# Corner order in the small products, and three bank sets in place of four in chunk 0, of an attention and SiLU-MLP kernel

## The chip, the cores and the metric

The kernel runs on one core of one Trainium2 chip. The metric is the device time of one execution in microseconds (us), as the median of several runs.

## The reference

Two stages follow each other. The first is linear attention: softmax of q over the features of a head, softmax of k over the sequence, and two products without any further softmax. Its output, with the heads side by side, is the input x of a two-layer network with SiLU between the layers.

```python
batch, n_heads, seq, head_dim = (8, 8, 576, 64)
q_s = softmax(q, axis=-1); k_s = softmax(k, axis=2)
kv  = np.einsum('bhsd,bhse->bhde', k_s, v)        # 64 x 64 per head
att = np.einsum('bhsd,bhde->bhse', q_s, kv)
x   = att.transpose(0, 2, 1, 3).reshape(4608, 512)
h   = x @ w_in                                     # 512 -> 2048
g   = h * (1.0 / (1.0 + np.exp(-h)))
out = g @ w_out                                    # 2048 -> 512
```

## The kernel before

**Tiling.** The 4608 rows of x are worked in chunks t. Chunk 0 is the 576 rows of batch 0; chunk 1 has 448 rows (64 more of its second product are copied from chunk 0); chunks 2 to 8 have 512. A chunk goes through three steps: the attention of its batch (b), the first product with W1 and SiLU into GT, and the second product with W2 into the output tile ow. From chunk 1 on the first product is made with a seven-product (Strassen) scheme, `group(t, g, i)`, and from chunk 1 on so is the second one, `prod(t, i, m)`. Chunk 0 is made plainly: the first product by `wide_mm` and `wide_silu`, one feature block of 128 at a time (fb 0 to 15), the second by `mm2_plain`, four matmuls for each of 16 steps. Eight feature blocks of chunk 1 are made plainly too, by `mm1`.

**Attention.** `exp_q`, `qsum`, `qnorm` make the softmax of q, `exp_k` the exponentials of k, `vcast` puts v into `vaug` with a column of ones beside each head, so that `kv` gives the product and the normalizing sum at once. q is transposed by TensorE (`tr`, `trcopy`) for batches 0 and 1, by a DMA (`q_transpose`) afterwards. The tiles of `kv` and `xt_mm` are 64x64: each matmul uses one of the four corners of the 128x128 array, with r and s choosing the half of the input partitions and the half of the output partitions. `kv` (line 189) makes 72 matmuls of 65 columns for a batch, in 18 rounds of four corners. `kvcopy` scales them into `kvn`; `xt_mm` (line 228) makes x's products, four corners for each piece, and `xt_evac` copies them from PSUM into XT.

**Memory for sums.** PSUM has eight banks, in the tile PS. Chunk 0's first product takes two banks for a feature block, banks 2 * (fb % 4) and the next: four sets. `wide_silu` reads them twice: ScalarE makes a tanh (line 250) into sg, VectorE multiplies (line 251) into GT. `mm2_plain` adds up in banks 2 to 5; `mm2_plain_out(0, m)` copies bank 2 + m out (lines 418 and 420). The groups of chunk 1 use banks 0, 1 and 6, 7, those of later chunks banks 0, 1 and 2, 3. `mm1` has one bank for a feature block.

**Order.** Everything is issued in an order written out by hand (`manual_schedule`). TensorE's work is a list `units`; `plan(u, f)` puts other work in front of unit u, so each engine's queue gets its instructions in the order in which the units are walked. After chunk 0's 16 `wide` units, from b1 on, come the units of `mm2_plain` (b0, "b"), then pairs of these with chunk 1's groups (gs, "g") by the string `four_pairs`, then eight `mm1` units, then chunk 2 (`full(2)`).

```python
    units += [b0.pop(0) for _ in range(10)]
    units += [{"b": b0, "g": gs}[x].pop(0) for x in four_pairs[:-1]]
    units += [lambda i=i: mm1(1, FB[i], (i + 2) % 4) for i in range(HF)]
```

**Loads.** W1, W2 and batch 1 are loaded on POOL's queue, in the order of the program; batch 0 and the batches from 3 on, and the stores, on SP's. A small POOL copy, `gate`, reads the first k load of batch 0 before W1 is loaded, and a second one (line 566) reads W1's second load before batch 1's q is. W1 comes in five loads: two halves (of input rows, c) of feature blocks 0 to 3, then blocks 4 to 7, 8 to 11 and 12 to 15.

Of the kernel before, what the change touches and what calls it, by code (L numbers as in the profile page):

```python
# [17 lines left out]
def kernel(  # L18
# [9 lines left out]
    nc = tc.nc  # L28
    B, H, S, D = q.shape
# [3 lines left out]
    J = S // P  # L33
    NG = H // 2
    NC = DM // 128
    NFB = DFF // 128
    HF = NFB // 2
    TCH = 512
# [66 lines left out]
    def exp_q(b, cc, g0=0, g1=2):  # L105
        if "eq" not in st[b]:
            st[b]["eq"] = ap.tile([128, J, NG * D], BF16, name="eq")
        nc.scalar.activation(  # L108
            out=half(st[b]["eq"], cc)[:, :, g0:g1], in_=jgd(b, "qt", cc)[:, :, g0:g1], func=ACT.Exp
        )  # L110

    def exp_k(b, cc):
        nc.scalar.activation(out=half(ek, cc), in_=jgd(b, "kt", cc), func=ACT.Exp)  # L113
# [30 lines left out]
    def qsum(b, cc, gs=None):  # L144
        new_zq(b)
        z, e = st[b]["zq"][:, cc], half(st[b]["eq"], cc)
        if gs is None:
            nc.vector.reduce_sum(out=z, in_=e, axis=AX.X)  # L148
        else:
            nc.vector.reduce_sum(out=z[:, :, gs], in_=e[:, :, gs, :], axis=AX.X)  # L150
        if gs != 0:
            nc.vector.reciprocal(out=st[b]["rzq"][:, cc], in_=z)  # L152
# [19 lines left out]
    def tr(b, cc, j0, j1, bank):  # L172
        t = PS[:, bank, :].bitcast(BF16)
        for j in range(j0, j1):
            nc.tensor.transpose(
                out=t[:, (j - j0) * 128:(j - j0 + 1) * 128],
                in_=st[b]["eq"][:, j, cc * 128:(cc + 1) * 128],
                identity=ident,
            )

    def trcopy(b, cc, j0, j1, bank, eng=nc.vector):
        t = PS[:, bank, :].bitcast(BF16)[:, 0:(j1 - j0) * 128].rearrange("x (j y) -> x j y", y=128)
        copy(eng, new_qt(b)[:, j0:j1, cc, :], t)

    def kv(b, cc):
        for j in range(J):
            for r in range(2):
                for s in range(2):
                    nc.tensor.matmul(  # L189
                        out=PS[s * 64:(s + 1) * 64, 6 + r, cc * 128:cc * 128 + E1],  # L190
                        lhsT=ek[r * 64:(r + 1) * 64, j, (2 * cc + s) * D:(2 * cc + s + 1) * D],
                        rhs=vaug[r * 64:(r + 1) * 64, j, 2 * cc + s, :],
                        start=(j == 0),
                        stop=(j == J - 1),
                    )
# [13 lines left out]
    def kv_both(b):  # L209
        kv(b, 0)  # L210
        kv(b, 1)
        kvcopy(b)
# [9 lines left out]
        return got  # L222

    def xt_mm(b, cc, col, n, bank, dst):
        for r in range(2):
            for s in range(2):
                h = slice(s * 64, (s + 1) * 64)
                nc.tensor.matmul(  # L228
                    out=PS[r * 64:(r + 1) * 64, bank + s, dst:dst + n],
                    lhsT=kvn[b % 3][h, cc, r, :],  # L230
                    rhs=st[b]["qT"][h, col // P:(col + n) // P, cc, r * 64:(r + 1) * 64],
                )
# [5 lines left out]
    def xt(t, cc, eng=nc.scalar):  # L238
        got = pieces(t)
        for b, col, n, dst in got:  # L240
            xt_mm(b, cc, col, n, 6, dst)
        xt_evac(t, cc, 6, got[0][3], TCH, got[0][3], eng)
# [12 lines left out]
    def wide_mm(fb, cs, ns=range(2)):  # L255
        for c in cs:
            for n in ns:
                nc.tensor.matmul(  # L258
                    out=PS[:, 2 * (fb % 4) + n, 0:S // 2],
                    lhsT=W1[:, c, fb * 128:(fb + 1) * 128],  # L260
                    rhs=XTS[0][:, c, n * (S // 2):(n + 1) * (S // 2)],
                    start=(c == 0),
                    stop=(c == NC - 1),
                )

    def wide_silu(fb):
        bank = 2 * (fb % 4)
        silu(
            0, fb, PS[:, bank:bank + 2, 0:S // 2],
            GTS[0][:, fb, :].rearrange("p (a n) -> p a n", a=2), S,  # L270
        )
# [12 lines left out]
    def mm1(t, fb, bank):  # L284
        o0 = pieces(t)[0][3]
        mm1_mm(t, fb, bank, range(NC))
        nc.scalar.activation(  # L287
            out=GTS[t % 2][:, fb, o0:TCH], in_=PS[:, bank, o0:TCH], func=ACT.Silu, scale=1.0 / XS
        )
# [21 lines left out]
    def ws_op(i, g):  # L311
        w, f0, f1 = WS[g], 4 * g + 8, 4 * g
        in0, in1, op = {
            1: (wa(0, f1), wa(1, f1), ALU.add),
            2: (w[0], wa(0, f0), ALU.subtract),
            3: (wa(0, f0), wa(0, f1), ALU.subtract),
            4: (wa(1, f0), w[1], ALU.subtract),
        }[i]
        nc.vector.tensor_tensor(out=w[i - 1], in0=in0, in1=in1, op=op)

    def xs_op(t, i):
        x = [xs[:, :, 0:width(t)] for xs in XS4]
        in0, in1 = {
            1: (xb(t, 0, 1), xb(t, 0, 0)),
            2: (xb(t, 1, 1), x[0]),
            3: (xb(t, 1, 1), xb(t, 0, 1)),
            4: (xb(t, 1, 0), x[1]),
        }[i]
        nc.vector.tensor_tensor(out=x[i - 1], in0=in0, in1=in1, op=ALU.subtract)
# [114 lines left out]
    def t_op(i, eng, f0=0, f1=HF):  # L444
        o, in0, in1 = {
            1: (T1, B12, B11),
            2: (T2, B22, T1),
            3: (T3, B22, B12),
            4: (T4, B21, T2),
        }[i]  # L450
        f = slice(f0, f1)
        eng.tensor_tensor(out=o[:, f], in0=in0[:, f], in1=in1[:, f], op=ALU.subtract)
# [91 lines left out]
    def load_w1(f0, f1, c0=0, c1=NC):  # L544
        nc.gpsimd.dma_start(
            out=W1[:, c0:c1, f0 * 128:f1 * 128],
            in_=w_in[c0 * 128:c1 * 128, f0 * 128:f1 * 128].rearrange("(c p) f -> p c f", p=128),
        )
# [12 lines left out]
    load_w1(0, 4, 0, 2)  # L561
    load_w1(0, 4, 2, 4)
    load_w1(4, 8)
    load_w1(8, 12)
    load_w1(12, 16)
    nc.gpsimd.tensor_copy(gate, W1[0:1, 2, 0:1])
    load(1, "qt", q, 0, nc.gpsimd)
    load(1, "qt", q, 1, nc.gpsimd)
    load_w2(0, 4)
# [36 lines left out]
    xt_evac(0, 1, 6, 0, 320, 0, nc.scalar)  # L606
    xt_evac(0, 1, 2, 0, 256, 320, nc.vector)
    wide_mm(1, (0, 1))
    wide_mm(2, (0, 1))


    units = []
# [2 lines left out]
    def plan(u, f):  # L615
        at.setdefault(u, []).append(f)

    def wide(fb):
        wide_mm(fb, range(2 if fb < 3 else 0, NC))
        wide_silu(fb)  # L620

    for fb in range(NFB):
# [19 lines left out]

    b0 = [lambda i=i: mm2_plain(0, i) for i in range(NFB)]
    gs = [lambda i=i: group(1, 1, i, None, True) for i in ORDER]
    units += [b0.pop(0) for _ in range(10)]
    units += [{"b": b0, "g": gs}[x].pop(0) for x in four_pairs[:-1]]
    units += [lambda i=i: mm1(1, FB[i], (i + 2) % 4) for i in range(HF)]
    assert not (b0 or gs)

    def full(t):  # L650
# [117 lines left out]
    plan(13, lambda: (exp_q(1, 1, 1, 2), qsum_pair(1, 1), qnorm(1, 0, nc.gpsimd)))  # L768
    plan(14, lambda: (load(2, "qt", q, 0, nc.gpsimd), load(2, "qt", q, 1, nc.gpsimd)))
    plan(b1 + 2, lambda: (exp_k(1, 0), exp_k(1, 1)))  # L770
    plan(b1 + 4, lambda: (tr(1, 0, 0, 5, 6), tr(1, 0, 5, J, 7)))
    plan(b1 + 4, lambda: (trcopy(1, 0, 0, 5, 6, nc.scalar), trcopy(1, 0, 5, J, 7)))
    plan(b1, lambda: (qsum_end(1, 1), qnorm(1, 1, nc.vector)))
    plan(b1, lambda: load_w2(12, 16))
    plan(b1 + 9, lambda: nc.scalar.copy(out=GTS[1][:, :, 0:64], in_=GTS[0][:, :, TCH:S]))
    plan(b1 + 3, lambda: (load(2, "kt", k, 0, nc.gpsimd), load(2, "kt", k, 1, nc.gpsimd)))
    plan(b1 + 6, lambda: (load(2, "vt", v, 0, nc.gpsimd), load(2, "vt", v, 1, nc.gpsimd)))
    plan(b1 + 4, lambda: vcast(1, 0, nc.scalar))
    plan(b1 + 5, lambda: (tr(1, 1, 0, 5, 0), tr(1, 1, 5, J, 1)))
    plan(b1 + 5, lambda: (vcast(1, 1, nc.scalar, 0, 1), vcast(1, 1, nc.vector, 1, 2)))  # L780
    plan(b1 + 6, lambda: (trcopy(1, 1, 0, 5, 0, nc.scalar), trcopy(1, 1, 5, J, 1)))
    plan(b1 + 8, lambda: kv_both(1))
    plan(b1 + 9, lambda: xt(1, 0))
    plan(b1 + 10, lambda: xt(1, 1))

    plan(b1 + 3, lambda: (ws_op(1, 1), ws_op(2, 1)))
    plan(b1 + 4, lambda: ws_op(3, 1))
    plan(b1 + 6, lambda: ws_op(4, 1))
    plan(b1 + 9, lambda: t_op(1, nc.vector))
    plan(b1 + 11, lambda: (xs_op(1, 1), ws_op(1, 0)))  # L790
    plan(b1 + 11, lambda: (xs_op(1, 2), xs_op(1, 3), xs_op(1, 4)))
    plan(b1 + 11, lambda: exp_q(2, 0))
    plan(b1 + 12, lambda: (qsum(2, 0, 0), qsum(2, 0, 1), qnorm(2, 0, nc.gpsimd)))
    plan(b1 + 14, lambda: exp_q(2, 1))
    plan(b1 + 15, lambda: exp_k(2, 0))
    plan(b1 + 15, lambda: (qsum(2, 1, 0), qsum(2, 1, 1), qnorm(2, 1, nc.gpsimd)))
    plan(b1 + 16, lambda: q_transpose(2))
    plan(b1 + 18, lambda: exp_k(2, 1))
    plan(b1 + 18, lambda: (vcast(2, 0, nc.gpsimd), vcast(2, 1, nc.gpsimd)))
    plan(b1 + 22, lambda: (group_silu(1, 2, 4, 1), group_silu(1, 0, 12, 0)))  # L800
    plan(b1 + 19, lambda: t_op(2, nc.vector))
    plan(b1 + 23, lambda: [load(3, x, y, i, nc.sync) for x, y, i in (
        ("qt", q, 0), ("kt", k, 1), ("kt", k, 0), ("vt", v, 0), ("vt", v, 1), ("qt", q, 1)
    )])
    plan(b1 + 22, lambda: mm2_plain_out(0, 0, nc.vector))
    plan(b1 + 22, lambda: mm2_plain_out(0, 1, nc.vector))
    plan(b1 + 24, lambda: group_silu(1, 1, 12, 1))
    plan(b1 + 14, lambda: ws_op(2, 0))
    plan(b1 + 24, lambda: (t_op(4, nc.vector), ws_op(3, 0)))
    plan(b1 + 25, lambda: kv_both(2))  # L810
    plan(b1 + 26, lambda: ws_op(4, 0))
# [41 lines left out]
```

## Time and profile before

| what | value |
| --- | --- |
| median of 5 runs | 263.81 us (263.69 to 264.52) |
| the profiled execution's own time | 263.75 us |
| its span, first to last instruction | 262.0 us |
| mean granted TensorE clock | 0.999 |
| TensorE matmuls busy | 252.7 us (96%) |
| VectorE, ScalarE, POOL busy | 208.3, 187.1, 67.8 us |
| 576 k-v matmuls (line 189), one of them | 193 ns (median) |
| 128 of x's products (line 228), one of them | 294 ns (median) |

An instruction's row has its own duration; matmuls are pipelined, so many are in flight at once, and what a group of them costs is read from the start of its first one to the start of the next group. PE is TensorE, DVE is VectorE, ACT is ScalarE. "Idle before" an instruction comes with what ended the wait. Line numbers L... are those of the kernel before; in the changed kernel, lines behind `kv` move by one, and behind `xt_mm` by two up to the loads of W1.

### The profile page before, as it was taken

To read this page: it belongs to the slowest core of one execution; us is meant where nothing else is said; L and a number is where in the kernel's file an instruction comes from. 1 tells how busy PE (TensorE), PEld (TensorE's weight loads), DVE (VectorE), ACT (ScalarE), POOL (GpSimd) and SP (SyncE) were. 2 spreads that over 40 slices of the span, in tenths; PEclk is the share of its full clock that TensorE was granted. 3 is DMA by queue.
4 is the path that set the end of the run, shared out by engine and by line. 5 is a ranking of instruction groups with operands and counts; after the bars stand their busy time and mean duration, and the time that the engine had idled before them with its cause. 6 is when DMAs were issued, how large, how long until landed. Compare 5 with 4: busy or idle time off the path is not lost.

```text
span 262.0 us, 6411 instructions
## 1 busy us (share of the span) xinstructions
PE 252.7 (96%) x2732; PEld 203.1 (78%) x2732; DVE 208.3 (80%) x269; ACT 187.1 (71%) x211; POOL 67.8 (26%) x63
## 2 busy tenths in 40 slices
PE   8899999999999999999999999999999999999992
PEld 3467655755888888888888888888888888888881
DVE  2957897897997999799979997999798548855832
ACT  4857976897995799579957995799574748484610
POOL 1664790650560306030603060306000000000003
PEclk9999999999999999999999999999999999999999
DMA  7999999679979486957794869540434003400634
GB/s 249 337 194 297 300 325 336 237 159 334 372 292 217 124 220 237 180 158 191 267 225 116 221 236 181 160 94 3 90 72 91 3 0 67 95 3 1 137 66 120
DMA packets 35964, 45.89 MB, mean 175 GB/s; under 512 B 16208, under 2 KB 21008, under 8 KB 35936
## 3 DMA queue, kind: packets, MB, share of 16 engines
q1 hardware_dynamic: 29568, 33.69, 46.9%
q0 software_dynamic: 6128, 11.60, 17.1%
q8 instruction: 21, 0.34, 0.5%
q10 hardware_dynamic: 240, 0.20, 0.2%
q14 instruction: 7, 0.06, 0.1%
HBM read 36.70 MB, written 9.44 MB: 176 GB/s over the span
## 4 chain that ended last, share of the span: by engine, by line
PE 76%; DMA 8%; DVE 8%; ACT 2%; POOL 2%; issue 2%; SPq 0%; POOLq 0%; DVEq 0%; ACTq 0%
PE PS L468 34%; PE PS L368 32%; PE PS L405 4%; DMA qt<-in_q_dram 4%; DMA kt<-in_k_dram 2%; DMA W<-in_moe_w_in_dram 2%; PE PS L228 2%; PE PS L276 2%; PE PS L189 2%; DVE h L346 1%; DVE S L442 1%; DVE zq L148 1%; DVE GT L442 1%; DVE GT L251 1%; POOL out_dram L732 1%
## 5 line engine op out<-in xcount | busy, mean ns | idle before, releaser
L346 DVE TENSOR_TENSOR h<-PS,h 128x1024 f32<-128x1024 f32 (+1 forms) x45 | 53.9, 1199 | 13.4 <-ACT h L89 7.5
L468 PEld LDWEIGHTS <-GT 128*128 128x128 f16 x512 | 49.6, 98 | 6.9 <-issue 1.2
L368 PEld LDWEIGHTS <-WS 128*128 128x128 f16 x480 | 46.8, 98 | 6.8 <-issue 0.7
L468 PE MATMUL PS<-W,GT 128*128 128x256 f16 x384 | 49.1, 273 | 0.0
L368 PE MATMUL PS<-XS,WS 128*128 128x256 f16 (+1 forms) x360 | 46.3, 272 | 0.1
L352 ACT ACTIVATE GT<-h 128x1024 f16<-128x1024 f32 (+1 forms) x45 | 46.1, 1047 | 0.3 <-DVE h L346 0.3
L89 ACT COPY h<-PS 128x1024 f32<-128x1024 f32 (+1 forms) x35 | 35.1, 1004 | 14.1 <-PE PS L368 13.6
L157 POOL TENSOR_TENSOR eq<-eq,rzq 128x1152 bf16<-128x1152 bf16 x13 | 27.7, 2135 | 55.5 <-DVE rzq L152 55.5
L468 PEld LDWEIGHTS <-S 128*128 128x128 f16 x384 | 37.1, 98 | 5.6 <-issue 1.0
L368 PEld LDWEIGHTS <-W 128*128 128x128 f16 x360 | 34.7, 98 | 5.5 <-issue 1.3
L468 PE MATMUL PS<-T,S 128*128 128x256 f16 x256 | 32.7, 273 | 0.2 <-ACT h L89 0.2
L368 PE MATMUL PS<-XT,W 128*128 128x256 f16 (+1 forms) x240 | 29.6, 272 | 0.5 <-ACT GT L287 0.3
L352 ACT ACTIVATE GT<-PS 128x1024 f16<-128x1024 f32 (+1 forms) x15 | 15.3, 1017 | 18.9 <-PE PS L368 18.9
L91 POOL CAST vaug<-vt 128x1152 bf16<-128x1152 f32 x12 | 16.4, 1370 | 45.6 <-DMA vt<-in_v_dram 37.6
L108 ACT ACTIVATE eq<-qt 128x1152 bf16<-128x1152 f32 (+1 forms) x18 | 19.1, 1059 | 3.6 <-DMA qt<-in_q_dram 3.5
L732 POOL DMA_DIRECT2D out_dram<-ow x5 | 2.7, 546 | 72.5 <-DVE ow L717 72.5
L148 DVE TENSOR_REDUCE zq<-eq 128x18 f32<-128x1152 bf16 x12 | 16.1, 1344 | 3.8 <-ACT eq L108 3.8
L113 ACT ACTIVATE ek<-kt 128x1152 bf16<-128x1152 f32 x16 | 18.3, 1153 | 0.4 <-DMA kt<-in_k_dram 0.4
L468 PE MATMUL PS<-W,S 128*128 128x256 f16 x128 | 16.5, 273 | 0.0
L488 DVE SCALAR_TENSOR_TENSOR ow<-PS,sc 128x512 f32<-128x512 f32 x7 | 4.8, 691 | 14.4 <-ACT sc L484 14.4
L258 PE MATMUL PS<-XT,W 128*128 128x288 f16 x128 | 16.0, 286 | 0.2 <-DVE XT L91 0.2
L405 PE MATMUL PS<-W,GT 128*128 128x512 f16 x64 | 15.6, 379 | 0.2
(79 smaller groups left out, 343.5 us busy)
## 6 DMA issues: line engine op xcount, KB each, us to landing
out_dram<-ow SPq DMA_DIRECT2D x64, 128.0 KB, 2.4
qt<-in_q_dram SPq DMA_DIRECT2D x12, 576.0 KB, 5.1
kt<-in_k_dram SPq DMA_DIRECT2D x12, 576.0 KB, 5.7
vt<-in_v_dram SPq DMA_DIRECT2D x12, 576.0 KB, 5.3
qt<-in_q_dram POOLq DMA_DIRECT2D x4, 576.0 KB, 8.8
kt<-in_k_dram POOLq DMA_DIRECT2D x4, 576.0 KB, 12.1
vt<-in_v_dram POOLq DMA_DIRECT2D x4, 576.0 KB, 12.8
W<-in_moe_w_out_dram POOLq DMA_DIRECT2D x4, 512.0 KB, 13.3
```

The costliest lines, as they stand in the source:

```text
L89: eng.copy(out=o, in_=i)
L91: eng.tensor_copy(o, i)
L108: nc.scalar.activation(out=half(st[b]["eq"], cc)[:, :, g0:g1], in_=jgd(b, "qt", cc)[:, :, g0:g1], func=ACT.Exp)
L113: nc.scalar.activation(out=half(ek, cc), in_=jgd(b, "kt", cc), func=ACT.Exp)
L148: nc.vector.reduce_sum(out=z, in_=e, axis=AX.X)
L157: eng.tensor_tensor(out=e, in0=e, in1=r[:, :, :, None].to_broadcast([128, J, 2, D]), op=ALU.mult)
L258: nc.tensor.matmul(out=PS[:, 2 * (fb % 4) + n, 0:S // 2], lhsT=W1[:, c, fb * 128:(fb + 1) * 128], rhs=XTS[0][:, c, n * (S // 2):(n + 1) * ...
L346: nc.vector.tensor_tensor(out=four(t, i), in0=group_bank(t, True), in1=four(t, i), op=ALU.add)
L352: nc.scalar.activation(out=group_out(t, f, n), in_=x, func=ACT.Silu, scale=1.0 / XS)
L368: nc.tensor.matmul(out=PS[:, bank + p // 2, (p % 2) * HT:(p % 2) * HT + width(t)], lhsT=a[:, c, p * 128:(p + 1) * 128], rhs=bb[:, c, 0:wid ...
L405: nc.tensor.matmul(out=PS[:, 2 + tb, :], lhsT=GTS[t % 2][:, fc, tb * 128:(tb + 1) * 128], rhs=W2[:, fc, :], start=(fc == 0), stop=(fc == N ...
L468: nc.tensor.matmul(out=PS[:, bank, m * HN:(m + 1) * HN], lhsT=a[:, fc, m * 128:(m + 1) * 128], rhs=bb[:, fc, :], start=(first and fc == 0) ...
```

## The change

There are four parts.

- In `kv` and `xt_mm` the two loops over r and s become a loop over i and r with s = r ^ i: the corners with r = s come first, then those with r != s.
- Chunk 0's first product takes three sets of two banks (fb % 3); the first halves of two feature blocks rather than three are made ahead.
- W1's last half comes in two loads by halves of the input rows, each over feature blocks 8 to 15, instead of by feature blocks; the second `gate` copy goes.
- Nine `mm2_plain` units instead of ten stand ahead of the pairs, and the last one stands behind all groups. `mm1` uses banks i % 4. Most of what was planned from b1 + 4 to b1 + 19 is planned one unit earlier. The first two output copies of chunk 0 are planned one unit later, behind batch 3's loads, and the first of them is made by ScalarE instead of VectorE.

```diff
     def kv(b, cc):
         for j in range(J):
-            for r in range(2):
-                for s in range(2):
+            for i in range(2):
+                for r in range(2):
+                    s = r ^ i
                     nc.tensor.matmul(
...
     def xt_mm(b, cc, col, n, bank, dst):
-        for r in range(2):
-            for s in range(2):
+        for i in range(2):
+            for r in range(2):
+                s = r ^ i
                 h = slice(s * 64, (s + 1) * 64)
...
-                    out=PS[:, 2 * (fb % 4) + n, 0:S // 2],
+                    out=PS[:, 2 * (fb % 3) + n, 0:S // 2],
...
-        bank = 2 * (fb % 4)
+        bank = 2 * (fb % 3)
...
-    load_w1(8, 12)
-    load_w1(12, 16)
-    nc.gpsimd.tensor_copy(gate, W1[0:1, 2, 0:1])
+    load_w1(8, 16, 0, 2)
+    load_w1(8, 16, 2, 4)
...
-    wide_mm(2, (0, 1))
...
-        wide_mm(fb, range(2 if fb < 3 else 0, NC))
+        wide_mm(fb, range(2 if fb < 2 else 0, NC))
...
-    units += [b0.pop(0) for _ in range(10)]
-    units += [{"b": b0, "g": gs}[x].pop(0) for x in four_pairs[:-1]]
-    units += [lambda i=i: mm1(1, FB[i], (i + 2) % 4) for i in range(HF)]
+    units += [b0.pop(0) for _ in range(9)]
+    units += [{"b": b0, "g": gs}[x].pop(0) for x in four_pairs]
+    units += [lambda i=i: mm1(1, FB[i], i % 4) for i in range(HF)]
...
-    plan(b1 + 4, lambda: (tr(1, 0, 0, 5, 6), tr(1, 0, 5, J, 7)))
+    plan(b1 + 3, lambda: (tr(1, 0, 0, 5, 6), tr(1, 0, 5, J, 7)))
...
-    plan(b1 + 8, lambda: kv_both(1))
-    plan(b1 + 9, lambda: xt(1, 0))
-    plan(b1 + 10, lambda: xt(1, 1))
+    plan(b1 + 7, lambda: kv_both(1))
+    plan(b1 + 8, lambda: xt(1, 0))
+    plan(b1 + 9, lambda: xt(1, 1))
...
-    plan(b1 + 22, lambda: mm2_plain_out(0, 0, nc.vector))
-    plan(b1 + 22, lambda: mm2_plain_out(0, 1, nc.vector))
+    plan(b1 + 23, lambda: mm2_plain_out(0, 0, nc.scalar))
+    plan(b1 + 23, lambda: mm2_plain_out(0, 1, nc.vector))
```

More of the change, by code (lines that the diff above doesn't have):

```diff
@@ L770 @@
     plan(b1 + 2, lambda: (exp_k(1, 0), exp_k(1, 1)))
-    plan(b1 + 4, lambda: (tr(1, 0, 0, 5, 6), tr(1, 0, 5, J, 7)))
-    plan(b1 + 4, lambda: (trcopy(1, 0, 0, 5, 6, nc.scalar), trcopy(1, 0, 5, J, 7)))
+    plan(b1 + 3, lambda: (tr(1, 0, 0, 5, 6), tr(1, 0, 5, J, 7)))
+    plan(b1 + 3, lambda: (trcopy(1, 0, 0, 5, 6, nc.scalar), trcopy(1, 0, 5, J, 7)))
     plan(b1, lambda: (qsum_end(1, 1), qnorm(1, 1, nc.vector)))
     plan(b1, lambda: load_w2(12, 16))
-    plan(b1 + 9, lambda: nc.scalar.copy(out=GTS[1][:, :, 0:64], in_=GTS[0][:, :, TCH:S]))
+    plan(b1 + 8, lambda: nc.scalar.copy(out=GTS[1][:, :, 0:64], in_=GTS[0][:, :, TCH:S]))
     plan(b1 + 3, lambda: (load(2, "kt", k, 0, nc.gpsimd), load(2, "kt", k, 1, nc.gpsimd)))
@@ L788 @@
     plan(b1 + 6, lambda: ws_op(4, 1))
[L789 to L799, printed above, removed]
+    plan(b1 + 8, lambda: t_op(1, nc.vector))
+    plan(b1 + 10, lambda: (xs_op(1, 1), ws_op(1, 0)))
+    plan(b1 + 10, lambda: (xs_op(1, 2), xs_op(1, 3), xs_op(1, 4)))
+    plan(b1 + 10, lambda: exp_q(2, 0))
+    plan(b1 + 11, lambda: (qsum(2, 0, 0), qsum(2, 0, 1), qnorm(2, 0, nc.gpsimd)))
+    plan(b1 + 13, lambda: exp_q(2, 1))
+    plan(b1 + 14, lambda: exp_k(2, 0))
+    plan(b1 + 14, lambda: (qsum(2, 1, 0), qsum(2, 1, 1), qnorm(2, 1, nc.gpsimd)))
+    plan(b1 + 15, lambda: q_transpose(2))
+    plan(b1 + 17, lambda: exp_k(2, 1))
+    plan(b1 + 17, lambda: (vcast(2, 0, nc.gpsimd), vcast(2, 1, nc.gpsimd)))
     plan(b1 + 22, lambda: (group_silu(1, 2, 4, 1), group_silu(1, 0, 12, 0)))
-    plan(b1 + 19, lambda: t_op(2, nc.vector))
+    plan(b1 + 18, lambda: t_op(2, nc.vector))
     plan(b1 + 23, lambda: [load(3, x, y, i, nc.sync) for x, y, i in (
@@ L804 @@
     )])
-    plan(b1 + 22, lambda: mm2_plain_out(0, 0, nc.vector))
-    plan(b1 + 22, lambda: mm2_plain_out(0, 1, nc.vector))
+    plan(b1 + 23, lambda: mm2_plain_out(0, 0, nc.scalar))
+    plan(b1 + 23, lambda: mm2_plain_out(0, 1, nc.vector))
     plan(b1 + 24, lambda: group_silu(1, 1, 12, 1))
-    plan(b1 + 14, lambda: ws_op(2, 0))
+    plan(b1 + 13, lambda: ws_op(2, 0))
     plan(b1 + 24, lambda: (t_op(4, nc.vector), ws_op(3, 0)))
```

## The prediction, made before the changed kernel ran

> **What bounds the kernel now.** I read the page first, then TensorE's rows in order of time, then the chain of waits for 24 to 34 us, then VectorE's and ScalarE's rows of the places where TensorE stood still.
>
> ```profile
> span 262.0 us, 6411 instructions
> PE 252.7 (96%) x2732; PEld 203.1 (78%) x2732; DVE 208.3 (80%) x269; ACT 187.1 (71%) x211; POOL 67.8 (26%) x63
> ```
>
> The page says that TensorE is the bound: 96% busy. In the busy times by stretch its share from 84 to 244 us is 159.97 of 160.00 us, so what it gains or loses before 84 us reaches the end unchanged. Only the first 84 us have stalls to win. TensorE's rows in order of time (start, us, what, idle before and its releaser):
>
> ```profile
> 15.28 15.97 PE L258 MATMUL PS<-XT,W 128*128 128x288 f16 x128 [0.25 <-DVE XT L91]
> 31.38 3.84 PE L405 MATMUL PS<-W,GT 128*128 128x512 f16 x16
> ...
> 54.40 1.67 PE L276 MATMUL PS<-XT,W 128*128 128x448 f16 x8 [0.36 <-DVE ow L420]
> ...
> 62.37 0.60 PE L368 MATMUL PS<-XT,W 128*128 128x256 f16 x4
> 63.30 1.47 PE L368 MATMUL PS<-XT,W 128*128 128x256 f16 x12 [0.33 <-ACT GT L287]
> ...
> 102.95 0.80 PE L189 MATMUL PS<-vaug,ek 64*64 64x65 bf16 x72
> 103.69 1.05 PE L368 MATMUL PS<-XT,W 128*128 128x256 f16 x8
> ...
> 109.91 0.41 PE L228 MATMUL PS<-qT,kvn 64*64 64x256 bf16 x8
> 110.25 1.92 PE L468 MATMUL PS<-T,GT 128*128 128x256 f16 x16
> ```
>
> To see: chunk 0's first product (L258) runs without a stall; there are stalls at 54.40 and 63.30; and the small products of L189 and L228 last 0.74 and 0.34 us until the next line starts. The chain (start, us, what) shows why the second product starts haltingly:
>
> ```profile
> 28.47 0.81 POOL h L129
> ...
> 30.06 1.94 DVE GT L251 x3
> 32.00 0.04 issue
> 32.04 2.10 PE PS L405 x9
> ```
>
> **Corners.** Nothing is added; 576 k-v matmuls and 128 of x's products are reordered. L258's matmuls start every 122.5 ns for 288 columns, 0.425 ns a column. So 72 of 65 columns one by one would take 1.99 us; the row has 0.74 with entry and exit. Eight of 256 columns would take 0.87; the row has 0.34. All four corners already run abreast: in the trace four start 3 to 4 ns apart, with L189 stepping along a row first and L228 along a column first, both with a diagonal step in the middle. The diagonal order has no other steps. I take 0. Bounds: k-v rounds of four start every 31.6 ns on average against 27.6 of columns, so 4.0 x 144 rounds = 0.6 us is the most to win there, and some 25 ns at each of 14 pairs of rounds of L228, 0.35; a gain of 0.9. If only two ran abreast, rounds would rise by 23.6 ns (3.4 us over 144), and L228's 9216 columns by 0.425 ns each (3.9): a loss of 7.3.
>
> The Trainium skill ("TensorE: Matmul & The Clock Gate", Part 3, The mechanism) says that a weight load overlaps running matmuls only where their row groups differ. That would favour this change: L189 loads two corners of one row group in turn. By it 36 loads a batch would each wait for a matmul of 193 ns, 6.9 us, and the change would win most of that eight times over; the 0.74 us of the row rules it out, and by the row the sum stays as it is.
>
> **Three sets of banks instead of four.** One feature block takes 8 x 122.5 = 0.98 us. Its last row ends 0.165 us later, the tanh (L250) starts 0.04 after that and lasts 0.65, the multiply (L251) starts 0.68 after the tanh and lasts 0.75: the banks are free 2.69 us after the block's start. With three sets they are wanted after 2.94: 0.25 of slack in the steady run, so nothing there. The exceptions: block 0 now ends its products at 16.88 (without block 2's half ahead), tanh 17.08, multiply 17.76 to 18.51, and block 3 wants the banks at 18.35: stall 0.20. Block 10's multiply ends at 28.35, block 13 wants its banks at 28.35: 0.04. Block 12's multiply stands behind qsum's end (L137, to 30.06), ends at 30.67, and block 15 wants it at 30.35: 0.36. Together 0.60; block 15 ends near 31.7. But the old stream then lost 0.29 in front of 31.38 and 0.23 in front of 32.04 for blocks 13 and 14's multiplies, which end as before (32.00). The new one gets to that third matmul at 32.12 instead of 32.04: a loss of **0.08**.
>
> **The last mm2_plain (4 matmuls, 0.86 us) behind the groups; all plans one unit earlier.** The transposes wanted at 35.06 are now wanted at 34.28; POOL's normalization (L157, 32.06 and 2.12 long) ends at 34.18, so they just fit. VectorE's queue of WS, vaug and qT (35.31 to 39.4) doesn't move up with them, so kvn is ready at about 40.6 where x's product would like 40.5: **+0.1**. The group work then runs about 0.66 earlier, not 0.86.
>
> **mm1 into banks 0 to 3 instead of 2, 3, 0, 1.** The stall at 54.40 is mm1 waiting for VectorE's ow copy out of bank 2, queued behind T (1.85 us). Now it wants bank 0, which ScalarE frees at 54.15 - 0.66 = 53.5; mm1 wants it at 53.87 + 0.2 = 54.07. Stall gone, start spacing back to normal: **-0.53**. At 62.37 and 63.30 the next group waits for the silus of the last two mm1s (excess spacing 0.18 and 0.49); these now sit in banks 2 and 3, wanted one group, 0.87 us, later: **-0.68**. The cover is ScalarE: it gets one ow copy (0.62) from VectorE, its last silu ends near 62.9, and bank 3 is wanted at 63.1. If that cover goes, the stall is back, up to 0.5.
>
> **SP and POOL queues.** SP issues batch 3's six loads before the stores instead of behind four (55.51 to 58.02): some 3 us earlier with the shift. Nobody waits for those stores. POOL's vaug casts move from 68.20 to about 65. Today they lie beside VectorE's S (L442: 2.05 us, its neighbour 1.21), in the VectorE chain that stalls TensorE by 0.08 at 73.76 and 0.30 at 81.00. So 0 to -0.38; I take **-0.2**.
>
> The Trainium skill ("SBUF — State Buffer", Who interferes with whom) says that a VectorE operation with two SBUF inputs contends with GpSimd's reads. That fits S, and speaks against the change too: the XS subtractions would meet the moved casts. Doubling their four rows of 0.42 would cost 1.7 on VectorE; by it the sum would be 0.2 to 0.3 smaller.
>
> **W1's last half and the gate.** The same bytes in two loads, cut by input rows instead of by features. In the landing records the last two loads land at 21.13 and 23.73, all on one queue in order. Until now block 12 (27.17) was the first to need the second one; now it is block 8's third chunk: 23.74 + 0.20 = 23.94. It just fits: 0, with +1 for each us that it is late. The gate copy held batch 1's q loads (issued 15.86) until W1's second load had landed; without it they are issued from 12.5 on but stand behind W1 in the same queue: they land 1.48 behind W1 as before. I take 0; from -0.2 (an earlier landing lets ScalarE go on) to +1.0.
>
> **Sum** against the profiled execution (263.75, span 262.0, 1.75 around it; the median is 0.06 above): 0.08 + 0.1 - 0.53 - 0.68 - 0.2 = -1.2, so 262.55 in such a run and 262.6 as a median.
>
> **Rivals.** *The order of corners counts after all, for the worse*: if corners 1 and 3, which now differ from their neighbours in row and column, make the next one wait, +7.3 in full, 269.9; from a quarter of that (some 6 ns a round and a quarter of the columns) it outweighs the 1.2 and ends slower. For it: no row shows this exact order. Against: the same steps appear at 3 to 4 ns. Chance 0.15, all causes of slower included.
> *The cover is gone*: W1's last load lands 0.5 late and ScalarE's copy brings back 0.5 of the stall near 63: -1.2 + 0.5 + 0.5 = -0.2, 263.6, no change. For it: margins of 0.2 us in both places. Chance 0.18.
> *Diagonals also help*: rounds at 27.6 ns and no gap between L228's rounds: 0.6 to 0.9 more, 261.9. Chance 0.09.
> The forecast: 0.58.
>
> **Numbers.** About 0.2%, 0.53 us, is what a measurement of this kernel can tell from no change. Faster 0.67 (forecast and diagonals), same 0.18, slower 0.15. The range 261.9 to 264.1 takes in the forecast, the second rival and the third down to its edge, and leaves out the slower cases. Forecast alone: 262.1 to 263.2.
>
> **What would show it.** Right: 72 k-v matmuls still near 0.74 us; short stalls in chunk 0's first product in front of blocks 3 and 15; no wait for ow near 53 to 54 us nor for a silu near 61 to 62; S near 1.2 us; everything after 84 us shifted by one amount. Wrong: k-v or x rows that are longer, a wait for a W DMA near 24 us, a ScalarE wait in front of t = 2's second group.

## The result and the profile after

The changed kernel runs in 263.38 us (median; 262.96 to 264.22) against 263.89 us for the kernel before on the same chip. The ratio is 0.998, with a 95% interval of 0.9974 to 0.9985: faster by about 0.5 us where 1.2 was forecast. That lies inside the wide range of the prediction (261.9 to 264.1) and outside the 262.1 to 263.2 that it gave to its forecast alone. The profiled execution took 263.38 us, its span 261.6.

From the page of the changed kernel:

```profile
span 261.6 us, 6410 instructions
PE 252.6 (97%) x2732; PEld 203.3 (78%) x2732; DVE 208.0 (80%) x268; ACT 187.6 (72%) x212; POOL 66.6 (25%) x62
```

TensorE's rows in order of time (start, us, what, idle before and its releaser):

```profile
15.54 15.21 PE L260 MATMUL PS<-XT,W 128*128 128x288 f16 x120 [0.25 <-DVE XT L91]
30.94 1.14 PE L260 MATMUL PS<-XT,W 128*128 128x288 f16 x8 [0.20 <-DVE GT L253]
...
54.29 1.68 PE L278 MATMUL PS<-XT,W 128*128 128x448 f16 x8
...
62.08 1.91 PE L370 MATMUL PS<-XT,W 128*128 128x256 f16 x16
...
70.28 1.05 PE L470 MATMUL PS<-T,S 128*128 128x256 f16 x8 [0.18 <-ACT h L89]
...
80.59 1.03 PE L370 MATMUL PS<-XS,WS 128*128 128x256 f16 x8 [0.49 <-DVE h L348]
...
102.54 0.80 PE L190 MATMUL PS<-vaug,ek 64*64 64x65 bf16 x72
103.27 1.05 PE L370 MATMUL PS<-XT,W 128*128 128x256 f16 x8
...
109.49 0.41 PE L230 MATMUL PS<-qT,kvn 64*64 64x256 bf16 x8
109.83 1.92 PE L470 MATMUL PS<-T,GT 128*128 128x256 f16 x16
```

To see: the waits at mm1's start and at chunk 2's first groups are gone, the rows of k-v and of x's products last 0.73 and 0.34 us as before, and chunk 0's first product has got the wait in front of block 15. But in front of 80.59 TensorE stands for 0.49 us, its groups being 1.53 apart where 0.87 is usual. The same place in the kernel before:

```profile
79.83 1.04 PE L468 MATMUL PS<-W,GT 128*128 128x256 f16 x8
81.00 1.03 PE L368 MATMUL PS<-XS,WS 128*128 128x256 f16 x8
```

There they are 1.17 apart: 0.30 us of spacing was lost before, 0.65 is lost now.

From start to start of the stages, the two executions and that of the experiment that settled the matter (e7, below):

| stretch of TensorE | before | after | e7 | forecast, after - before | measured |
| --- | --- | --- | --- | --- | --- |
| start to chunk 0's first product | 15.28 | 15.54 | 15.57 | 0 | +0.26 |
| from there to mm1 | 39.12 | 38.75 | 38.77 | -0.35 | -0.37 |
| from there to chunk 2 | 7.97 | 7.79 | 7.79 | -0.18 | -0.18 |
| from there to batch 4's k-v | 40.58 | 40.46 | 39.38 | -0.70 | -0.12 |
| from there to the last matmul | 153.73 | 153.72 | 153.73 | 0 | -0.01 |

The first row is the arrival of batch 0's loads, which both kernels make alike; over all the profiles here it lies between 15.22 and 15.80. In these two executions the rows below it agree with the forecast to 0.02 us, but for one. For the row up to mm1 that is partly luck: e1, e6 and e11, which differ from the kernel before in nothing that should touch it, took 39.16, 39.40 and 38.87 us there. The row that is off runs from chunk 2's start at 62 us to batch 4's k-v at 103 us: there 0.58 us are missing. This row scatters little, 40.58 us in the kernel before and in e1.

VectorE's and then POOL's rows of this stretch, in the kernel before:

```profile
67.69 1.21 DVE L442 TENSOR_TENSOR S<-GT 128x2048 f16<-128x2048 f16 x1
68.94 2.05 DVE L442 TENSOR_TENSOR S<-S,GT 128x2048 f16<-128x2048 f16 x1
...
75.59 0.27 DVE L152 RECIPROCAL rzq<-zq 128x18 f32<-128x18 f32 x1
...
76.85 2.35 DVE L442 TENSOR_TENSOR GT<-GT 128x2048 f16<-128x2048 f16 x1
```

```profile
68.20 3.81 POOL L91 CAST vaug<-vt 128x1152 bf16<-128x1152 f32 x2 [12.34 <-DMA vt<-in_v_dram]
73.13 2.12 POOL L157 TENSOR_TENSOR eq<-eq,rzq 128x1152 bf16<-128x1152 bf16 x1 [1.11 <-DVE rzq L152]
76.00 2.12 POOL L157 TENSOR_TENSOR eq<-eq,rzq 128x1152 bf16<-128x1152 bf16 x1 [0.76 <-DVE rzq L152]
```

And in the changed kernel:

```profile
66.92 1.22 DVE L444 TENSOR_TENSOR S<-GT 128x2048 f16<-128x2048 f16 x1
68.17 2.06 DVE L444 TENSOR_TENSOR S<-S,GT 128x2048 f16<-128x2048 f16 x1
...
74.82 0.27 DVE L152 RECIPROCAL rzq<-zq 128x18 f32<-128x18 f32 x1
...
76.08 2.71 DVE L444 TENSOR_TENSOR GT<-GT 128x2048 f16<-128x2048 f16 x1
```

```profile
65.11 1.16 POOL L91 CAST vaug<-vt 128x1152 bf16<-128x1152 f32 x1 [9.70 <-DMA vt<-in_v_dram]
67.09 2.06 POOL L91 CAST vaug<-vt 128x1152 bf16<-128x1152 f32 x1 [0.81 <-DMA vt<-in_v_dram]
...
75.59 2.12 POOL L157 TENSOR_TENSOR eq<-eq,rzq 128x1152 bf16<-128x1152 bf16 x1 [1.48 <-ACT GT L354]
```

The first cast moved out of the way, the second did not: v's second load landed at 66.94, and the cast met S again. S still takes 2.06 us, where the prediction's sign of being right was "S near 1.2 us". The subtraction into GT, 1.21 us when nothing runs on POOL, takes 2.71 instead of 2.35, because POOL's normalization now starts 0.5 us ahead of it rather than 0.85. VectorE comes to the reciprocal and to GT 0.77 us earlier than before, just as TensorE comes 0.77 us earlier to the place where it then waits (79.06 for 79.83). The normalization alone comes only 0.41 us earlier: it starts 0.50 us after the end of the reciprocal (75.09 to 75.59), in the kernel before 0.14 us after it (75.86 to 76.00).

### The profile page after: what moved, and what is told of

Its sections match the earlier page's. It is cut to its first block, busy times and chain, and to the rows that moved or that the text cites. A ratio compares the mean times of both kernels' runs of the same rounds, so it can differ in the third digit from the quotient of the medians.

```text
span 261.6 us, 6410 instructions
## 1 busy us (share of the span) xinstructions
PE 252.6 (97%) x2732; PEld 203.3 (78%) x2732; DVE 208.0 (80%) x268; ACT 187.6 (72%) x212; POOL 66.6 (25%) x62
## 4 chain that ended last, share of the span: by engine, by line
PE 82%; DVE 7%; DMA 4%; ACT 2%; POOL 2%; issue 1%; SPq 1%; POOLq 0%; DVEq 0%; ACTq 0%
PE PS L470 34%; PE PS L370 33%; PE PS L407 5%; DMA vt<-in_v_dram 4%; PE PS L260 3%; PE PS L278 2%; PE PS L230 2%; PE PS L190 2%; DVE h L348 1%; DVE S L444 1%; DVE GT L444 1%; DVE zq L148 1%; SPq L97 1%; POOL out_dram L732 1%; DVE GT L253 1%
## 5 line engine op out<-in xcount | busy, mean ns | idle before, releaser
L370 PEld LDWEIGHTS <-W 128*128 128x128 f16 x360 | 34.7, 98 | 4.8 <-issue 0.5
L91 POOL CAST vaug<-vt 128x1152 bf16<-128x1152 f32 x12 | 15.8, 1318 | 44.2 <-DMA vt<-in_v_dram 43.9
L260 PEld LDWEIGHTS <-W 128*128 128x128 f16 x128 | 12.4, 98 | 4.3 <-issue 1.3
```

What stands on the lines that cost most here:

```text
L91: eng.tensor_copy(o, i)
L260: nc.tensor.matmul(out=PS[:, 2 * (fb % 3) + n, 0:S // 2], lhsT=W1[:, c, fb * 128:(fb + 1) * 128], rhs=XTS[0][:, c, n * (S // 2):(n + 1) * ...
L370: nc.tensor.matmul(out=PS[:, bank + p // 2, (p % 2) * HT:(p % 2) * HT + width(t)], lhsT=a[:, c, p * 128:(p + 1) * 128], rhs=bb[:, c, 0:wid ...
```

## Experiments

Each was timed beside the kernel before. The ratio is to the kernel before, with its 95% interval. Line numbers are those of each kernel.

**Corners alone, and everything but the corners.**

```diff
 # e1: the kernel before, in kv and xt_mm; e2 is the changed kernel with the reverse
-            for r in range(2):
-                for s in range(2):
+            for i in range(2):
+                for r in range(2):
+                    s = r ^ i
```

> The kernel before with only the order of the corners changed (r = s first) in the k-v and x products. Theory (corners run abreast in any order): 72 k-v matmuls still 0.74 us to the next line, eight of x's products 0.34, time within 0.2 us of the kernel before. Rival (the corners took back part of the expected gain): the rows are longer and the kernel is 0.3 to 0.7 us slower than before.

> The changed kernel with the old order of the corners. Theory: the same as the changed kernel, 0.5 us under the kernel before, within 0.2. Rival (the corners cost time): 0.3 to 0.7 us faster than the changed kernel, so 0.8 to 1.2 under the kernel before.

Measured: e1 263.99 us, ratio 0.9997 (0.9988 to 1.0006); e2 263.38 us, ratio 0.9973 (0.9965 to 0.9982). The rows of e1:

```profile
103.09 0.81 PE L190 MATMUL PS<-vaug,ek 64*64 64x65 bf16 x72
103.83 1.05 PE L370 MATMUL PS<-XT,W 128*128 128x256 f16 x8
...
110.05 0.41 PE L230 MATMUL PS<-qT,kvn 64*64 64x256 bf16 x8
110.39 1.81 PE L470 MATMUL PS<-T,GT 128*128 128x256 f16 x15
```

0.74 and 0.34 us in either order. The corners, which name the change, are worth nothing that these runs can tell (e1's interval is -0.3 to +0.2 us); what moves the time lies in the other edits.

**mm1's banks alone.**

```diff
 # e4: the kernel before
-    units += [lambda i=i: mm1(1, FB[i], (i + 2) % 4) for i in range(HF)]
+    units += [lambda i=i: mm1(1, FB[i], i % 4) for i in range(HF)]
```

> The kernel before with mm1's bank alone changed from (i + 2) % 4 to i % 4; loads, corners, sets and plans stay. Theory (this edit carries the whole change): the waits at 62.37 and 63.30 go (0.68 us), that at 54.40 shrinks by about 0.2 (ScalarE frees bank 0 only at 54.15), and about 0.9 arrives at 71 us; of that VectorE's subtraction of GT beside GpSimd's normalization near 76 to 79 us takes back 0.3 to 0.4, so 263.4 in the end, ratio 0.998. Rival 1 (the prediction's sum): nothing is taken back, 263.0, ratio 0.9965. Rival 2: the plans one unit earlier are needed with it, and the edit alone gives nothing, 263.9.

Measured: 263.31 us, ratio 0.9972 (0.996 to 0.9984). The time is that of the theory, but the way to it is not. TensorE's, ScalarE's, VectorE's and POOL's rows, one fence each:

```profile
54.34 1.67 PE L276 MATMUL PS<-XT,W 128*128 128x448 f16 x8 [0.16 <-ACT GT L352]
...
75.75 1.03 PE L368 MATMUL PS<-XT,W 128*128 128x256 f16 x8 [1.04 <-ACT GT L352]
```

```profile
72.20 1.16 ACT L108 ACTIVATE eq<-qt 128x1152 bf16<-128x1152 f32 x1 [1.68 <-DMA qt<-in_q_dram]
73.38 1.28 ACT L352 ACT_TABLE_LOAD   x1
74.68 1.02 ACT L352 ACTIVATE GT<-PS 128x1024 f16<-128x1024 f32 x1
```

```profile
68.41 1.22 DVE L442 TENSOR_TENSOR S<-S,GT 128x2048 f16<-128x2048 f16 x1
```

```profile
68.49 2.16 POOL L91 CAST vaug<-vt 128x1152 bf16<-128x1152 f32 x1 [12.48 <-DMA vt<-in_v_dram]
```

The waits of 62 and 63 us are gone, and that at 54.34 has shrunk to 0.16. But batch 3's q, still loaded behind the stores, landed at 72.18 (68.41 in the changed kernel), ScalarE's exponential waited for it, then the table and the silu, and TensorE stood for 1.04 us. In this execution the banks' gain was so lost a stage later, for want of SP's new order. But the execution took 263.75 us, and nine of the twelve were faster. By the medians this one line brings as much as the whole change (ratio 0.9972 against 0.998, and the intervals overlap). So how often q comes too late stays open, and with it what SP's new order is worth on average. And here S began 0.08 us ahead of the cast and kept its 1.22 us, while the cast took 2.16 instead of 1.16.

**Without POOL's second normalization of batch 3.** In both kernels the normalization of the second half of batch 3's q is left out.

```diff
 # e5: the changed kernel; e6: the kernel before
-            plan(u + (16, 17)[i], lambda i=i: qnorm(b, i, nc.gpsimd))
+            if not (b == 3 and i == 1):
+                plan(u + (16, 17)[i], lambda i=i: qnorm(b, i, nc.gpsimd))
```

> The changed kernel without POOL's normalization of batch 3's second half of q (that half stays unnormalized). Theory (VectorE's GT subtraction at 76 us takes 2.7 us because POOL's normalization runs beside it, and TensorE waits 0.49 us for what is queued behind it): GT falls to about 1.2 us, the wait at 80.6 us goes, everything behind is 0.6 us earlier, 1.0 to 1.1 under the kernel before. Rival (TensorE's wait at 80.6 has another cause, the delay came from the loads or from the three bank sets): GT stays over 2 us or the wait stays, time within 0.2 of the changed kernel.

> The kernel before, without POOL's normalization of batch 3's second half of q (that half stays unnormalized). Theory: GT falls from 2.35 to 1.2 us, TensorE's wait of 0.13 at 81.0 us goes, 0.3 us faster than the kernel before; against the changed kernel without it the difference is then 0.7 to 1.0 us, near the forecast. Rival: no change, and the difference between the two stays at 0.5.

Measured: e5 262.8 us, ratio 0.9957 (0.9943 to 0.9971); e6 263.98 us, ratio 0.999 (0.9975 to 1.0004). Between the two medians lie 1.2 us, as much as had been forecast for the change, but not term by term: S beside the casts was still stretched in both (2.00 and 2.06 us). e6 gained 0.1 us by its median, inside the noise, where 0.3 was expected; its trace does show the 0.28 (GT 1.21 us, no wait near 81, 40.30 us from chunk 2's start to batch 4's k-v instead of 40.58). VectorE's row of e5, and its largest wait on TensorE:

```profile
76.60 1.21 DVE L444 TENSOR_TENSOR GT<-GT 128x2048 f16<-128x2048 f16 x1
```

```profile
24.66 3.60 PE L260 MATMUL PS<-XT,W 128*128 128x288 f16 x28 [0.45 <-DMA W<-in_moe_w_in_dram]
```

GT's subtraction is back at 1.21 and the wait near 80.6 is gone. The second row is another matter: in this execution W1's last load landed at 24.62 (23.41 in the changed kernel's profile), later than the 23.94 of the prediction, and TensorE waited 0.45 us. From chunk 0's first product to mm1 this execution, the slowest of its five, took 39.63 us, 0.88 more than the changed kernel's. This part of the second rival does occur.

**Four sets of banks again; W1's old loads again.**

```diff
 # e3: the changed kernel; also wide_mm(2, (0, 1)) ahead of the units, and fb < 3 in wide
-                    out=PS[:, 2 * (fb % 3) + n, 0:S // 2],
+                    out=PS[:, 2 * (fb % 4) + n, 0:S // 2],
 # e8: the changed kernel
-    load_w1(8, 16, 0, 2)
-    load_w1(8, 16, 2, 4)
+    load_w1(8, 12)
+    load_w1(12, 16)
+    nc.gpsimd.tensor_copy(gate, W1[0:1, 2, 0:1])
```

> The changed kernel with chunk 0's first product back on four sets of two banks and three half blocks ahead. Theory (the prediction's term of 0.08): TensorE's waits in front of blocks 3 and 15 (0.22 and 0.36 us in the trace of after) go, and as much comes back as waits in front of the second product for the multiplies of the last blocks (0.29 and 0.23 in the trace of before); net 263.3, ratio to the kernel before 0.998. Rival: the three sets cost their full 0.58 us, because the second product now starts one unit later and the multiplies are done by then; then 262.8, ratio 0.996.

> The changed kernel with W1's last half loaded as before, cut by features, and with the gate copy ahead of batch 1's q loads. Theory (the loads as such cost nothing): 263.4, ratio 0.998. Rival (the last load lands later than 23.9 us in a good part of the executions, and TensorE then waits in block 8): 0.1 to 0.3 us less, 263.1 to 263.3, ratio 0.997, and the spread of the times gets smaller.

Measured: e3 263.24 us, ratio 0.9972 (0.9961 to 0.9982); e8 263.15 us, ratio 0.9966 (0.9952 to 0.9979). Both intervals overlap that of the changed kernel, so the times decide neither. In the traces the three sets cost 0.21 us: from chunk 0's first product to mm1 it is 38.75 us with three and 38.54 with four (38.54 in e9 too). With W1's old loads a late execution costs as much, only elsewhere. TensorE's row of e8, then ScalarE's:

```profile
28.40 1.89 PE L260 MATMUL PS<-XT,W 128*128 128x288 f16 x13 [0.50 <-DVE GT L253]
```

```profile
26.34 0.68 ACT L108 ACTIVATE eq<-qt 128x576 bf16<-128x576 f32 x1 [0.69 <-DMA qt<-in_q_dram]
```

W1's last load landed at 24.84 there, batch 1's q behind it at about 26.3, and ScalarE's exponential of q held up the tanh of a feature block. What the loads cost on average stays open.

Something else in e8 matters more. Its GT takes 2.35 us again, and from chunk 2's start to batch 4's k-v it needs 40.10 us, 0.36 less than the changed kernel:

```profile
76.87 2.35 DVE L444 TENSOR_TENSOR GT<-GT 128x2048 f16<-128x2048 f16 x1
```

**Keeping the second cast away from S.**

```diff
 # e7: the changed kernel
+            if b == 3 and i == 1:
+                plan(u + 11, lambda: nc.gpsimd.tensor_copy(gate, SS[2][0:1, 0, 0:1]))
             plan(u + (2, 11)[i], lambda i=i: vcast(b, i, nc.gpsimd))
```

> The changed kernel with one copy of a single element on GpSimd that reads VectorE's third S before the second vaug cast of batch 3, so that this cast starts only after VectorE's two S. Theory (what ate the gain is VectorE's queue beside GpSimd between 67 and 79 us): the S that took 2.06 us beside the cast takes 1.22, VectorE comes to the subtraction of GT some 0.8 us earlier, the wait of 0.49 us near 80.6 goes, and the time falls by 0.4 to 0.65 to 262.7 to 263.0, ratio to the kernel before 0.995 to 0.997. Rival 1: the subtraction of GT, which runs beside GpSimd's normalization whatever its start, still ends as late, because it waits for the matmuls of GT's group and not for S: wait and time as in the changed kernel, 263.4, ratio 0.998. Rival 2: the later cast delays the normalization on GpSimd's queue or the k-v products, and time is lost: over 263.6.

Measured: 262.42 us, ratio 0.9935 (0.9921 to 0.995), 0.96 us less than the changed kernel and below the theory's 262.7 to 263.0. VectorE's rows, POOL's, TensorE's:

```profile
66.96 1.22 DVE L444 TENSOR_TENSOR S<-GT 128x2048 f16<-128x2048 f16 x1
68.21 1.23 DVE L444 TENSOR_TENSOR S<-S,GT 128x2048 f16<-128x2048 f16 x1
...
75.30 2.35 DVE L444 TENSOR_TENSOR GT<-GT 128x2048 f16<-128x2048 f16 x1
```

```profile
69.50 0.18 POOL L673 CAST gate<-S 1x1 f32<-1x1 f16 x1 [3.91 <-DVE S L444]
69.63 1.15 POOL L91 CAST vaug<-vt 128x1152 bf16<-128x1152 f32 x1
...
74.45 2.12 POOL L157 TENSOR_TENSOR eq<-eq,rzq 128x1152 bf16<-128x1152 bf16 x1 [1.12 <-DVE rzq L152]
```

```profile
69.99 1.04 PE L470 MATMUL PS<-T,S 128*128 128x256 f16 x8
...
79.56 1.04 PE L370 MATMUL PS<-XS,WS 128*128 128x256 f16 x8
```

S takes 1.23, VectorE's chain is 0.8 us earlier, and both waits are gone, although GT's subtraction still takes 2.35 us: with that lead it is hidden. (It was 2.71: the normalization starts 0.14 us after its reciprocal here, so e7 took away the late start as well as the stretched S.) The row of 69.99 also corrects the profile's releaser. The wait in front of 70.28 was put down to ScalarE's copy of h; here that copy ends at 70.32 (it starts at 69.31 and lasts 1.01), and TensorE does not wait for it. What released TensorE at 70.28 was S, which ended at 68.17 + 2.06 = 70.23.

**The same in the kernel before.** Both casts of batch 3 wait for S.

```diff
 # e11: the kernel before
+            if b == 3 and i == 0:
+                plan(u + 11, lambda: nc.gpsimd.tensor_copy(gate, SS[2][0:1, 0, 0:1]))
-            plan(u + (2, 11)[i], lambda i=i: vcast(b, i, nc.gpsimd))
+            plan(u + (11, 11)[i], lambda i=i: vcast(b, i, nc.gpsimd))
```

> The kernel before with both vaug casts of batch 3 put behind VectorE's second S, by a copy of a single element on GpSimd that reads it; nothing else is changed. Theory (the bound of 0.38 in the prediction's term for the queues was right as a price of S beside the casts): S takes 1.22 in place of 2.05 us, the waits at 73.76 and 81.00 (0.08 and 0.30 us of lost spacing) go, 263.5 to 263.6, ratio 0.9986. Rival: the subtraction of GT beside the normalization sets that wait alone, and 264.0 stays, ratio 1.000.

Measured: 263.81 us, ratio 0.9986 (0.9969 to 1.0003); its executions scatter from 262.86 to 265.21, and the time alone decides nothing. The trace does: S 1.23, no wait at 71, 73.8 or 81, and 39.87 us from chunk 2's start to batch 4's k-v instead of 40.58. So the kernel before lost 0.71 us in this chain, not the 0.38 that the prediction counted from two of its three waits: the one at 71.05, where the groups start 1.21 us apart for 0.87, adds 0.34.

**Keeping the normalization away from GT.**

```diff
 # e12: the changed kernel
+            if b == 3 and i == 1:
+                plan(u + 17, lambda: nc.gpsimd.tensor_copy(gate, blk(t - 1, 0, 1)[0:1, 0, 0:1]))
             plan(u + (16, 17)[i], lambda i=i: qnorm(b, i, nc.gpsimd))
```

> The changed kernel with a copy of a single element on GpSimd that reads the new GT ahead of batch 3's second normalization, so that it starts only after VectorE's subtraction of GT; S beside the casts stays slow (2.06). Theory (the normalization is what stretches the subtraction): GT takes 1.21 in place of 2.71 us, the wait of 0.49 near 80.6 goes, 262.7 to 262.9, ratio to the kernel before 0.9955. Rival: the normalization, now about 1.7 us later, keeps batch 3's transposes and x's products waiting, and what is won is lost again: 263.4.

Measured: 267.6 us, ratio 1.0134 (1.0115 to 1.0152). GT took 1.21 and the wait near 80.6 went, as the theory had it, but the rival won by far more than its price. TensorE's rows, and the busy times by stretch (from and to, us, then busy us of PE, PEld, DVE, ACT and POOL, the granted clock, DMA share, GB/s):

```profile
85.91 0.33 PE L230 MATMUL PS<-qT,kvn 64*64 64x320 bf16 x4 [2.92 <-DMA qT<-eq]
86.17 2.52 PE L470 MATMUL PS<-T,GT 128*128 128x256 f16 x16
88.48 1.91 PE L370 MATMUL PS<-XS,W 128*128 128x256 f16 x8
```

```profile
86.00:88.50 2.50, 2.50 (x21) 1.88 (x21) 1.22 (x1) 0.00 (x0) 1.14 (x1) 0.77 0.69 272
88.50:91.50 3.00, 3.00 (x19) 2.28 (x18) 0.69 (x1) 1.06 (x2) 1.18 (x2) 0.62 0.29 64
```

The normalization ended at 79.67 instead of 77.71, and the transposing DMA behind it landed at 85.87 instead of 82.38. TensorE stood for 2.92 us, and for the 5.5 us behind that its granted clock was 0.77 and 0.62, which cost (1 - 0.77) x 2.5 + (1 - 0.62) x 3.0 = 1.7 us more.

**The old banks in the changed order, and all that helped in one.**

```diff
 # e10: e7 with
-    units += [lambda i=i: mm1(1, FB[i], i % 4) for i in range(HF)]
+    units += [lambda i=i: mm1(1, FB[i], (i + 2) % 4) for i in range(HF)]
 # e9: e7 with e3's four sets and e8's loads
```

> The changed kernel with the one-element copy ahead of batch 3's second vaug cast (which alone ran in 262.42) and with mm1's banks back at (i + 2) % 4. Theory (the prediction's terms of 0.53 and 0.68 for mm1's banks are the whole gain of the change): the waits for ow near 54 and for a silu near 62 to 63 come back, 1.2 us, 263.6, ratio to the kernel before 0.998. Rival: the plans one unit earlier and the earlier loads remove a good part of these waits by themselves; then half comes back, 263.0.

> The changed kernel with three edits: the one-element copy ahead of batch 3's second vaug cast, the four sets of two banks in chunk 0's first product, and W1's last half loaded as before. Theory (the gains stand side by side, from the medians of the single edits against the changed kernel: 0.96, 0.14 and 0.23 us): 262.1, ratio to the kernel before 0.9925, no wait of TensorE over 0.1 us between 34 and 240 us but that at 43.7. Rival: the last two are noise, 262.4, ratio 0.9935.

Measured: e10 264.68 us, ratio 1.0024 (1.0012 to 1.0037); e9 262.27 us, ratio 0.9929 (0.9913 to 0.9944). In e10 TensorE's and ScalarE's rows are:

```profile
56.28 1.67 PE L278 MATMUL PS<-XT,W 128*128 128x448 f16 x8 [1.46 <-ACT ow L420]
...
65.18 1.47 PE L370 MATMUL PS<-XT,W 128*128 128x256 f16 x12 [0.33 <-ACT GT L289]
```

```profile
55.64 0.59 ACT L420 ACTIVATE ow<-PS 128x512 f32<-128x512 f32 x1
```

e10 is slower than both of its guesses (263.6 and 263.0). In the new order ScalarE frees bank 2 behind three silus, at 56.2. With the old banks mm1 wants that bank first and waits 1.46 us, four times what it waited in the kernel before: the reorder without the banks is a loss, even with e7's copy in it. e9 is the fastest version here, by 1.9 us against the kernel before; from e7 (0.9935) it can't be told apart.

## Why the prediction was right in sign and wrong in size

**Corners, 0:** right; e1 and e2 show it from both sides. The two rivals on the corners fall. The measured 263.38 lies nearer to the 263.6 of the second rival (the cover is gone) than to the forecast, but not by its mechanism: in the profile of after, W1's last load landed in time (23.41) and no wait for a silu came back.

**Three sets, +0.08:** the two waits came as worked out (0.22 for 0.20, 0.36 for 0.36), but with four sets the changed order would have lost 0.28 us in front of the second product, not 0.52, so the term is about 0.2. (The steps of a block add up to 2.62 us, as the rows of before have it, not to 2.69; with 0.32 of slack in place of 0.25 nothing else changes.) **Plans one unit earlier, +0.1:** both terms and the wait for bank 2 together were to give -0.35 up to mm1, and gave -0.37. With 0.21 for the three sets and -0.53 for bank 2 the plans are left with about -0.05: two misses, 0.13 and 0.15, cancel, and both are smaller than the scatter of this row.

**mm1's banks, -0.53 and -0.68:** right, all three waits are gone, and ScalarE's cover held. That price holds against the old order; in the new one the old banks cost 2.3 us (e10 against e7).

**SP and POOL queues, -0.2:** this is the step that failed; it measured +0.37 (40.46 - 40.58 = -0.12 for the stretch, of which -0.49 is the wait at 63.30). It took VectorE's chain to get shorter. From the copy of h that TensorE releases (66.55 us before, 65.78 after) to the h that TensorE waits for, VectorE works almost without a gap: 14.41 us before, 14.75 after, so 0.34 longer. TensorE's lost spacing at the end of that chain grew from 0.30 to 0.65 us. Two rows account for it, each about one part of the missing 0.58:

- S was to lose some of its 0.83 us beside the casts, worth the 0.2. It lost nothing (2.06). The prediction moved both casts "to about 65" as if only the plan held them, though the second one waits for v's second load, which landed at 66.94.
- GT, VectorE's other stretched row, was never asked about. It grew by 0.36 us, because POOL's normalization started late (see below). In e8, where it starts in time, the step measures +0.01 (40.10 - 40.58 + 0.49): what is left is that S gave nothing. e5 and e12 show that it is GT that makes TensorE wait near 80.6: in both GT takes 1.21 us and the wait is gone, though S is as slow as ever.

The prediction also left out the wait at 71.05, which the profile puts down to ScalarE and which e7 and e11 show to be S's. So a freed S was worth more than it allowed: with S freed and the normalization in time (e7) the stretch takes 39.38 us, 1.08 less than in the changed kernel, the missing 0.58 and 0.5 beyond what was forecast.

The Trainium skill ("SBUF — State Buffer", Who interferes with whom) covers the mechanism, and says that issue order decides which of the two stands still. The prediction cited the section for S and for XS only. The runs agree with it: the cast that began 0.08 us after S took 2.16 and S 1.22 (e4); the S that began 1.08 us after a cast took 2.06. Applied to every pair of VectorE and POOL rows between 65 and 80 us, it would have pointed to GT as well.

**SP's loads** were counted at nothing, since "nobody waits for those stores". True of the stores; but with TensorE earlier the loads become due, and e4's profiled execution lost 1.04 us for want of that edit.

**W1's last half and the gate, 0:** the load just fits in the profile of after and misses by 0.45 us in that of e5; the average is open. But taking the gate copy out has a side that the prediction did not see, and it is where GT's 0.36 us seem to come from. A normalization of batch 3 that starts some 0.5 us after its reciprocal, rather than 0.14, stands in seven of the fourteen traces. In before, e1, e6 and e8 it is the first of the two (72.63 to 73.13 in before), beside which VectorE runs nothing with two operands in SBUF, so it does no harm there. In after, e2 and e3 it is the second, and GT pays. Counted among the rows that the trace keeps of POOL, its waits included, the late one is the 69th in all seven. In e5, e7, e9, e10 and e11 no normalization of this batch is the 69th; in e4 and e12 one is, but it follows directly on other work of POOL; and none of these is late. The gate copy and its wait are two rows ahead of this place, and without them the second normalization moves onto it. e8 puts them back, with the old loads, and the 0.36 us are gone; so in these traces this term was nearer to +0.36 than to 0. **What stays open:** why that place is late, and whether the count alone decides it, since no run changes nothing but the count.

## What to carry to other kernels

When TensorE's waits are removed, follow the next engine in its chain to the next place where TensorE needs it, and the neighbours that slow this engine down: the gain ends where one of them does not move up too. Here VectorE moved up by 0.77 us and POOL's normalization beside it by 0.41. Look in the rows of before for instructions that take longer than their like, and ask what runs beside each; one copy of a single element that orders two such neighbours brought 0.96 us here, twice the whole change (part of it by the normalization's timely start). And when a step is moved, look up when its data land, not only what stands in front of it in the program.

## What the runs showed of the hardware

A VectorE operation with two operands in SBUF and a POOL operation that reads SBUF hardly overlap: GT's subtraction lost 1.14 us where it ran 1.27 us beside the normalization, and 1.50 us where it ran 1.63 us beside it. The one that began first kept its time in every pair of these traces whose starts lie 0.07 us or more apart. And in the one trace with a stop of 2.92 us in mid-run (e12), TensorE's granted clock was 0.77 and 0.62 for some 5.5 us behind it, another 1.7 us; behind waits of up to 1.46 us (e10) it stayed at 1.00.
